# Attention scores split 640 to 640 between the two halves of TensorE's rows, a second use for the value bank, and the even chunks' value products moved behind two later down products

## The chip, the cores and the metric

The kernel runs on one core of a Trainium2 chip. The core has a matrix engine (TensorE, PE in the profile; its weight loads are listed apart as PEld) and three element-wise engines: VectorE (DVE), ScalarE (ACT) and GpSimd (POOL). SyncE (SP) issues all the transfers that matter here. Each engine works through its own list of instructions in order, and engines wait for each other on semaphores. TensorE writes only to PSUM, which has eight banks of 128 partitions by 512 fp32 values. The metric is the device time of one launch in microseconds (us), the median of several runs; lower is better.

## The reference

x is 2048 tokens of 576 features. One half of the model is attention with a compressive memory: 32 heads of 18 features, the sequence cut into four segments of 512 tokens; the other half is a GEGLU feed-forward network with 4608 hidden features. A sigmoid gate per token mixes the two.

```python
for s in range(N):                                   # N = 4 segments of L = 512
    qs, ks, vs = q[:, :, s], k[:, :, s], v[:, :, s]
    logits = jnp.einsum("bhqd,bhkd->bhqk", qs, ks) * scale + mask
    p = _softmax(logits, axis=-1)
    a_dot = jnp.einsum("bhqk,bhkd->bhqd", p, vs)
    ...                                              # memory read: num / den
    o = g * a_mem + (1.0 - g) * a_dot
    outs.append(o)
    ...                                              # memory update
a = concat(outs) @ wo
b = (_gelu(x @ w_gate) * (x @ w_up)) @ w_down
return sigmoid(gate) * a + (1 - sigmoid(gate)) * b
```

The mask is causal inside a segment.

## The kernel before

**Stages.** The first stretch (to about 225 us) projects q, k, v, builds the memories and stores q, k and v in DRAM. The main loop then runs 72 steps (`step(v)`, line 1104), each of some 18.4 us, which carry feed-forward and attention side by side. A tail forms the last down products and the output projection. Every fp32 value is carried as a pair of fp16 words, high and low, so that a product of two values is three matmuls.

**A step's feed-forward part.** Step `v` treats hidden block `f = v // 2` and token pair `p = v % 2`. Gate and up projections of two 512-token chunks are formed with a Strassen-like scheme in three accumulators, each a bank of its own: `V`, `X` (bank `G`) and `Y` (bank `U`). `product` (line 1025) is six matmuls of 512 columns; `rest` (line 1032) and `low_rests` (line 1037) add the last 64 features, the latter with two 64-row products side by side on the two halves of TensorE's rows. Between products, VectorE copies or adds an accumulator (lines 1127, 1130, 1162, 1181, 1189) and ScalarE applies the gelu. `hidden` (line 1007) multiplies gate and up values on VectorE; it is put off to the start of the next step by `end_pair` (line 1096), which goes through the list `ends` (gate accumulator `X` first, then `Y`). A step also makes eight *down products* of the hidden block before (`down`, line 977: six matmuls of 288 columns, line 985, into a `dn` bank, then one VectorE instruction, line 993, that adds the bank to the accumulator `acc`; "eviction" below). Five of them are called `early` (`early[0]` to `early[4]`), three `late`; they stand between the products.

**A step's attention part.** A chunk is one head of one segment: 512 queries by 512 keys. Steps 2 to 65 start two chunks each, the even one `2k` and the odd one `2k + 1`, with `k = v - 2`. `scores` (line 876) forms the causal score rows of a chunk in four blocks of 128 queries: block `qi` sees `(qi + 1) * 128` keys, so its matmul (line 888) has 128, 256, 384 or 512 columns. Queries and keys hold 54 rows (three times 18), and they lie twice in SBUF, at rows 0 and at rows 64, so that one block's product can use the upper half of TensorE's rows while another uses the lower. `put(a, i)` has VectorE add the mask, copy a block out of PSUM and keep the row maximum (line 896). When all blocks are out, ScalarE forms the exponentials (`powers`), ScalarE and GpSimd split them into fp16 pairs (`pair_rows`), and SP turns them by transposing transfers (`turn_rows`, line 926, into `pt`, two buffers). `values(a)` multiplies them with the values, 20 matmuls of 37 columns (line 940) into the bank `pv`; one bank holds the even and the odd chunk of a pair. `normalize` (lines 950 to 957, VectorE) reads it out.

**Order.** The main loop's order on TensorE, VectorE, ScalarE and GpSimd is the order of the calls in `step`; nothing reorders it.

**Banks.** All eight PSUM banks are given out: `G`, `U`, `V` and `pv` once each, `st` and `dn` as pools of two, taken in turn. A tile in a bank waits until the tile before it in the same bank has been read. `spare()` (line 58) gives the down products `dn` in the main loop.

Of the kernel before, what the change touches and what calls it, by code (L numbers as in the profile page):

```python
# [13 lines left out]
OP = mybir.AluOpType  # L14
# [4 lines left out]
P = 128  # L19
# [3 lines left out]
DH = 18  # L23
L = 512
# [18 lines left out]
def kernel(ctx: ExitStack, tc: tile.TileContext, xs, wqk, wv, wo, wgu, wd, beta, out):  # L43
    nc = tc.nc
    pe, act, dve, pool, sp = nc.tensor, nc.scalar, nc.vector, nc.gpsimd, nc.sync
# [6 lines left out]
    def bank(tag, bufs=1, dt=F32):  # L52
        return ps.tile([P, 512 if dt == F32 else 1024], dt, name=tag, tag=tag, bufs=bufs)
# [319 lines left out]
    mask = cst.tile([P, L], BF16, name="mask")  # L373
# [16 lines left out]
    with tc.tile_pool(name="prj", bufs=2, side="right", reuse_waits="tile") as pp:  # L390
# [203 lines left out]
        with tc.manual_schedule(engines=ORDERED):  # L594
# [3 lines left out]
            start = bank("G")  # L598
# [175 lines left out]
            for s in range(4):  # L774
                p = s - 1
                if s:
                    for q in range(4):
                        pv = vrows(s, q, 0)
# [12 lines left out]
                        pv = vrows(s, q, 1)  # L791
# [41 lines left out]
    with tc.tile_pool(name="keep", bufs=2, side="right", reuse_waits="tile") as kp, ExitStack() as tail:  # L833
        home.update(d=kp)
        turns.update(of=2)
        hp, qts, kts, vts, obs, mx, prob = {}, {}, {}, {}, {}, {}, {}
# [34 lines left out]

        COL = [0, P, 3 * P, 6 * P, 10 * P]

        PIECES = (((3,), 0), ((2, 0), 64), ((1,), 0))

        def scores(a):

            k, e = divmod(a, 2)
            q, kt = qts[k], kts[k]
            mx[a] = ap_.tile([P, 4], F32, name="mx", bufs=2)  # L880
            prob[a] = ap_.tile([P, 10 * P], F32, name="pf", bufs=2)
            put = []
            for qis, r in PIECES:
                o = bank("dn", 2) if qis == (1,) else bank("st", 2)
                spots, off, h = [], 0, slice(r, r + 3 * DH)
                for qi in qis:
                    n = (qi + 1) * P
                    pe.matmul(o[:, off : off + n], q[h, e * L + qi * P : e * L + (qi + 1) * P],  # L888
                              kt[h, e * L : e * L + n], start=True, stop=True)
                    spots.append((qi, o[:, off : off + n]))  # L890
                    off += n
                put.append(spots)

            def piece(i):
                for qi, ov in put[i]:
                    dve.tensor_tensor_reduce(prob[a][:, COL[qi] : COL[qi + 1]], ov, mask[:, L - (qi + 1) * P :],  # L896
                                             1.0, -3e38, OP.add, OP.max, mx[a][:, qi : qi + 1])

            return piece

# [27 lines left out]
        def values(a):  # L928
            kk, e = divmod(a, 2)
            if e == 0:  # L930
                pvb[kk] = bank("pv")
            o = pvb[kk]
            pr = turned_p.pop(a)
            v = vts[kk // 4]
            c0 = (kk % 4) * VC
            for qi in range(4):
                ov = o[:, (4 * e + qi) * VC : (4 * e + qi + 1) * VC]
                for kb in range(qi + 1):
                    for i in range(2):
                        pe.matmul(ov, pr[:, 10 * i + COL[qi] // P + kb], v[:, 4 * e + kb, c0 : c0 + VC],  # L940
                                  start=kb == 0 and i == 0, stop=kb == qi and i == 1)
# [62 lines left out]
        def hidden(f, c, o, t):  # L1004

            sc = scl[f // 2][0]
            dve.scalar_tensor_tensor(t, o, sc[:, 6 + c : 7 + c], t, OP.mult, OP.mult)  # L1007
# [86 lines left out]
        ends, puts = [], {}  # L1094

        def end_pair():

            for g in ends:
                hidden(*g)
            for f, c, o, g in ends:  # L1100
                hidden_pair(f, c, g)
            ends.clear()

        def step(v):

            f, p = divmod(v, 2)
            fb, i4 = divmod(v, 4)
            c, e = 2 * p, 2 * p + 1
            k = v - LAG
            on = lambda i: 0 <= i < 2 * H  # L1110
            early = range(8 * i4, 8 * i4 + 5)
            late = range(8 * i4 + 5, 8 * i4 + 8)
            some = lambda b, js: chains(b, js) if b >= 0 else None
            put = lambda a, i: puts[a](i) if a in puts else None
# [11 lines left out]
            g1 = gl_tile()  # L1126
            dve.tensor_copy(g1, V)
            product(X, f, A11, x1, 0, 4, True)
            put(2 * k - 1, 0)
            dve.tensor_copy(Y, X)  # L1130
            if v == 0:
                last_sum(1, 1)
            if v == 1:
                scale_result()
            some(fb - 1, early[:1])
            put(2 * k - 1, 1)
            put(2 * k - 1, 2)
            puts.pop(2 * k - 1, None)
            if on(k - 2):
# [23 lines left out]
            if not fb:  # L1163
                dve.tensor_tensor(g0, V, g0, OP.add)
                gelu(f, c, g0, g0)
            some(fb - 1, early[1:2])
            if v == 0 or fb and i4 == 1:
                scales(fb + 1)
                scales_out(fb + 1)
# [8 lines left out]
                low_rests(f, (V, G4, x1), (Y, G4, x2_))  # L1178
            if on(k):
                puts[2 * k] = scores(2 * k)  # L1180
            dve.tensor_tensor(g1, Y, g1, OP.add)  # L1181
            gelu(f, e, g1, g1)
            if v == 3:
                for n in range(2):
                    high_d(n)
                    low_d(n)
            put(2 * k, 2)
            if fb:
                dve.tensor_tensor(g0, V, g0, OP.add)
                gelu(f, c, g0, g0)  # L1190
            if on(k - 1) and fb:
                values(2 * k - 2)
            some(fb - 1, early[3:4])
            put(2 * k, 0)
            some(fb - 1, early[4:])
            put(2 * k, 1)
            puts.pop(2 * k, None)
            if v < 3:
                ahead[v + 1] = first_product(v + 1)
# [14 lines left out]
            some(fb - 1, late[:1])  # L1214
            if low is not None:
                result_low(low)
            some(fb - 1, late[1:])
            if on(k - 1) and not fb:
                values(2 * k - 2)
            if fb:  # L1220
                low_rests(f, (X, U4, x1), (Y, UG, x2_))
                ends.append((f, c, X, g0))
# [106 lines left out]
```

## Time and profile before

| | |
|---|---|
| device time, median of 3 runs | 1612.17 us (1610.71 to 1613.14) |
| the profiled execution's own time | 1610.65 us |
| its span, first to last instruction | 1608.9 us |
| TensorE busy | 1596.7 us, 99% of the span |
| VectorE / ScalarE / GpSimd busy | 71% / 72% / 70% |
| mean granted TensorE clock | 0.998 |
| score matmuls (line 888) | 512 in 128 chunks |
| value matmuls (line 940) | 2560 in 128 chunks |
| evictions of a `dn` bank (line 993) | 534, mean 516 ns |

Times in the timeline are microseconds from the start of the span. A timeline row gives start, duration, engine, line, operation, the tile written and the tiles read, the shape and the count; where equal instructions follow each other they are merged, and a row's start is that of the first. Brackets at the end give the idle time before the row and what ended it. The end of a matmul is modelled and overlaps the next one's start, so the distance from one matmul's start to the next one's is what TensorE spends on it.

### The profile page before, as it was taken

What the parts mean: (1) busy time and instruction counts of PE and PEld (TensorE: products, weight loads), DVE (VectorE), ACT (ScalarE), POOL (GpSimd) and SP (SyncE); (2) the same over time, 40 slices, a digit from 0 to 9 for tenths busy, and PEclk for the clock granted to TensorE, in tenths of its full rate; (3) what the DMA queues carried; (4) which work ended last, traced back from release to release, by engine and by line L of the source; (5) the groups of instructions that cost most, each with busy time, mean ns of one, the idle gap of its engine ahead of it and who ended that gap; (6) DMA issues with size and microseconds to landing.
All of it is one profiled execution on the core that took longest, in us unless ns stands there. A gap on an engine that the chain in (4) does not pass through costs nothing.

```text
span 1608.9 us, 32610 instructions
## 1 busy us (share of the span) xinstructions
PE 1596.7 (99%) x11924; PEld 933.5 (58%) x11924; DVE 1140.2 (71%) x2940; ACT 1161.9 (72%) x1966; POOL 1133.1 (70%) x1093
## 2 busy tenths in 40 slices
PE   9999999999999999999999999999999999999999
PEld 5656754555555555555555555555555555555577
DVE  6665785677777777777777777777777777765543
ACT  6665445888888888888888888878888888864200
POOL 2233647798987888887979778888879797785200
PEclk9999999999999999999999999999999999999999
DMA  6532443788978797988988887978798887846251
GB/s 240 193 109 77 149 142 82 124 133 131 138 120 141 122 144 120 143 126 140 134 135 133 131 139 123 148 128 141 129 140 137 133 133 129 127 74 155 59 133 60
DMA packets 471872, 209.00 MB, mean 130 GB/s; under 512 B 427552, under 2 KB 436768, under 8 KB 471200
## 3 DMA queue, kind: packets, MB, share of 16 engines
q1 hardware_dynamic: 471712, 206.92, 71.6%
q8 instruction: 94, 1.54, 0.4%
q14 instruction: 66, 0.54, 0.1%
HBM read 90.99 MB, written 27.26 MB: 73 GB/s over the span
## 4 chain that ended last, share of the span: by engine, by line
PE 96%; DVE 1%; DMA 1%; POOL 1%; ACT 1%; issue 0%; SPq 0%; DVEq 0%; POOLq 0%
PE dn L985 26%; PE U L1025 17%; PE V L1025 12%; PE G L1025 11%; PE pv L940 4%; PE st L322 3%; PE st L312 3%; PE dn L322 2%; PE G L312 2%; PE U L1032 2%; PE st L888 2%; PE V L1037 1%; PE G L1037 1%; PE U L312 1%; PE G L1032 1%; PE V L1032 1%
## 5 line engine op out<-in xcount | busy, mean ns | idle before, releaser
L920 POOL TENSOR_TENSOR ph<-pf,ph 128x512 f16<-128x512 f32 (+1 forms) x256 | 354.2, 1405 | 176.9 <-ACT ph L919 175.0
L985 PE MATMUL dn<-paird,hh 128*128 128x288 f16 x3396 | 476.7, 286 | 0.9 <-POOL paird L305 0.9
L1025 PEld LDWEIGHTS <-pairg 128*128 128x128 f16 x3024 | 285.3, 98 | 309.9 <-issue 16.0
L985 PEld LDWEIGHTS <-hh 128*128 128x128 f16 x3456 | 332.3, 98 | 138.1 <-issue 2.6
L993 DVE SCALAR_TENSOR_TENSOR acc<-dn,ev,acc 128x288 f32<-128x288 f32 x534 | 274.0, 516 | 95.7 <-PE dn L985 86.9
L909 ACT ACTIVATE pf<-pf,mb,esc 128x512 f32<-128x512 f32 (+3 forms) x512 | 292.9, 642 | 6.7
L1025 PE MATMUL G<-x,pairg 128*128 128x512 f16 x864 | 209.9, 379 | 0.5 <-DVE gl L1007 0.5
L1025 PE MATMUL U<-xt,pairg 128*128 128x512 f16 x864 | 210.1, 379 | 0.0
L1012 POOL TENSOR_TENSOR hh<-gl,hh 128x512 f16<-128x512 f32 x144 | 164.0, 1160 | 56.0 <-ACT hh L1011 56.0
L896 DVE CUSTOM_DVE_ANT_0 pf<-st,mask 128x512 f32<-128x512 f32 (+2 forms) x384 | 184.0, 504 | 0.0
L293 POOL TENSOR_TENSOR pairg<-raw,pairg 128x640 f16<-128x640 f32 (+2 forms) x144 | 173.9, 1229 | 10.6 <-ACT pairg L289 10.6
L919 ACT ACTIVATE ph<-pf 128x512 f16<-128x512 f32 (+1 forms) x256 | 172.4, 720 | 0.0
L1162 DVE COPY gl<-U 128x512 f32<-128x512 f32 x72 | 49.8, 691 | 137.2 <-PE U L1025 137.2
L289 ACT ACTIVATE pairg<-raw 128x640 f16<-128x640 f32 (+2 forms) x144 | 89.5, 648 | 70.7 <-POOL raw L283 41.2
L258 POOL TENSOR_SCALAR raw<-raw,sc 128x640 f32<-128x640 f32 x72 | 135.0, 1889 | 0.0
L1015 ACT ACTIVATE gl<-gl,sc 128x512 f32<-128x512 f32 x144 | 98.3, 717 | 45.4 <-DVE gl L1181 25.2
L1025 PE MATMUL V<-x,pairg 128*128 128x512 f16 x432 | 106.0, 381 | 0.4 <-ACT hh L1011 0.2
L1181 DVE TENSOR_TENSOR gl<-U,gl 128x512 f32<-128x512 f32 x72 | 49.7, 691 | 79.8 <-PE U L1037 72.5
L1025 PE MATMUL V<-xt,pairg 128*128 128x512 f16 x432 | 105.7, 381 | 0.0
L1025 PE MATMUL U<-x,pairg 128*128 128x512 f16 x432 | 105.0, 379 | 0.4 <-DVE gl L1181 0.4
L1011 ACT ACTIVATE hh<-gl 128x512 f16<-128x512 f32 x144 | 82.9, 616 | 25.2 <-DVE gl L1007 25.1
L906 ACT ACTIVATE mb<-mx,esc 128x4 f32<-128x4 f32 x128 | 37.8, 295 | 85.8 <-DVE mx L896 83.1
(271 smaller groups left out, 2565.1 us busy)
## 6 DMA issues: line engine op xcount, KB each, us to landing
raw<-in_wgu_dram SPq DMA_DIRECT2D x36, 640.0 KB
rawd<-in_wd_dram SPq DMA_DIRECT2D x36, 288.0 KB
qk<-stage SPq DMA_DIRECT2D x36, 256.0 KB
qt<-qk SPq DMA_DIRECT2D x128, 72.0 KB
kt<-qk SPq DMA_DIRECT2D x128, 72.0 KB
vp<-vstage SPq DMA_DIRECT2D x16, 296.0 KB
vt<-vp SPq DMA_DIRECT2D x16, 296.0 KB
qt<-qk SPq DMA_DIRECT2D x128, 36.0 KB
```

The source lines that it names most:

```text
L258: pool.tensor_scalar(r, r, scl[f // 2][0][:, 0:1], None, OP.mult)
L293: pool.tensor_tensor(spot(f, *p, 1), raw_g[f][:, p[0] : p[1]], spot(f, *p, 0), OP.subtract)
L312: pe.matmul(o, w(k, a), x[:, 4 * b + k], start=n == 0, stop=False)
L896: dve.tensor_tensor_reduce(prob[a][:, COL[qi] : COL[qi + 1]], ov, mask[:, L - (qi + 1) * P :], 1.0, -3e38, OP.add, OP.max, mx[a][:, qi : q ...
L909: act.activation(r, r, AF.Exp, bias=b[:, qi : qi + 1], scale=esc[:, 0, c : c + 1])
L919: act.activation(h[:, 0, cols], p[:, cols], AF.Copy)
L920: pool.tensor_tensor(h[:, 1, cols], p[:, cols], h[:, 0, cols], OP.subtract)
L985: pe.matmul(o[:, :NH], hh[:, a, q * P : (q + 1) * P], w[:, b, n * NH : (n + 1) * NH], start=i == 0, stop=i == 5)
L993: dve.scalar_tensor_tensor(av, o[:, :NH], ev, av, OP.mult, OP.add)
L1012: pool.tensor_tensor(hh[:, 1], t, hh[:, 0], OP.subtract)
L1015: act.activation(t, o, AF.Gelu_apprx_tanh, scale=scl[f // 2][0][:, 2 + c : 3 + c])
L1025: pe.matmul(o, w[:, i, (a + k) * P : (a + k + 1) * P], x[:, b + k], start=start and k == 0 and i == 0 and b == h, stop=k == 1 and i == 1, ...
```

## The change

`PIECES` becomes a list of the four blocks with the row half and the bank of each for an even and an odd chunk. The 512-column block stays at rows 0 and the 384-column block at rows 64, each in an `st` bank. The 256-column block goes from rows 0 to rows 64 (bank `dn`, as before). The 128-column block goes from rows 64, where it shared an `st` bank with the 384-column block, to rows 0 and a bank of its own: `pv` in even chunks, `dn` in odd ones. `put` now takes a block's number instead of a piece's.

On VectorE, an odd chunk's 256- and 128-column blocks are read out in `end_pair`, between the two `hidden` instructions that the step before left over; an even chunk's 256-column block is read out ahead of the addition to `g1` (line 1181 before) instead of behind it, its 128-column block behind the addition to `g0`, and its 512- and 384-column blocks where pieces 0 and 1 stood.

On TensorE, `values(2k - 2)` moves from between the score products of chunk `2k` and `early[3]` to between `late[1]` and `late[2]`, from step 4 on. In step 4 alone (the fifth), `early[0]` moves back to stand directly ahead of `early[1]`.

```diff
--- before.py
+++ after.py
@@ -871,7 +871,7 @@
 
         COL = [0, P, 3 * P, 6 * P, 10 * P]
 
-        PIECES = (((3,), 0), ((2, 0), 64), ((1,), 0))
+        PIECES = ((3, 0, "st", "st"), (2, 64, "st", "st"), (1, 64, "dn", "dn"), (0, 0, "pv", "dn"))
 
         def scores(a):
 
@@ -879,22 +879,15 @@
             q, kt = qts[k], kts[k]
             mx[a] = ap_.tile([P, 4], F32, name="mx", bufs=2)
             prob[a] = ap_.tile([P, 10 * P], F32, name="pf", bufs=2)
-            put = []
-            for qis, r in PIECES:
-                o = bank("dn", 2) if qis == (1,) else bank("st", 2)
-                spots, off, h = [], 0, slice(r, r + 3 * DH)
-                for qi in qis:
-                    n = (qi + 1) * P
-                    pe.matmul(o[:, off : off + n], q[h, e * L + qi * P : e * L + (qi + 1) * P],
-                              kt[h, e * L : e * L + n], start=True, stop=True)
-                    spots.append((qi, o[:, off : off + n]))
-                    off += n
-                put.append(spots)
-
-            def piece(i):
-                for qi, ov in put[i]:
-                    dve.tensor_tensor_reduce(prob[a][:, COL[qi] : COL[qi + 1]], ov, mask[:, L - (qi + 1) * P :],
-                                             1.0, -3e38, OP.add, OP.max, mx[a][:, qi : qi + 1])
+            out = {}
+            for qi, r, *tags in PIECES:
+                n, h = (qi + 1) * P, slice(r, r + 3 * DH)
+                out[qi] = bank(tags[e], 1 if tags[e] == "pv" else 2)[:, :n]
+                pe.matmul(out[qi], q[h, e * L + qi * P : e * L + n], kt[h, e * L : e * L + n], start=True, stop=True)
+
+            def piece(qi):
+                dve.tensor_tensor_reduce(prob[a][:, COL[qi] : COL[qi + 1]], out[qi], mask[:, L - (qi + 1) * P :],
+                                         1.0, -3e38, OP.add, OP.max, mx[a][:, qi : qi + 1])
 
             return piece
 
@@ -1097,6 +1090,10 @@
 
             for g in ends:
                 hidden(*g)
+                if g is ends[0]:
+                    for qi in (1, 0):
+                        if puts:
+                            puts[max(puts)](qi)
             for f, c, o, g in ends:
                 hidden_pair(f, c, g)
             ends.clear()
@@ -1126,14 +1123,14 @@
             g1 = gl_tile()
             dve.tensor_copy(g1, V)
             product(X, f, A11, x1, 0, 4, True)
-            put(2 * k - 1, 0)
+            put(2 * k - 1, 3)
             dve.tensor_copy(Y, X)
             if v == 0:
                 last_sum(1, 1)
             if v == 1:
                 scale_result()
-            some(fb - 1, early[:1])
-            put(2 * k - 1, 1)
+            if v != 4:
+                some(fb - 1, early[:1])
             put(2 * k - 1, 2)
             puts.pop(2 * k - 1, None)
             if on(k - 2):
@@ -1163,7 +1160,7 @@
             if not fb:
                 dve.tensor_tensor(g0, V, g0, OP.add)
                 gelu(f, c, g0, g0)
-            some(fb - 1, early[1:2])
+            some(fb - 1, early[0 if v == 4 else 1 : 2])
             if v == 0 or fb and i4 == 1:
                 scales(fb + 1)
                 scales_out(fb + 1)
@@ -1178,22 +1175,21 @@
                 low_rests(f, (V, G4, x1), (Y, G4, x2_))
             if on(k):
                 puts[2 * k] = scores(2 * k)
+            put(2 * k, 1)
             dve.tensor_tensor(g1, Y, g1, OP.add)
             gelu(f, e, g1, g1)
             if v == 3:
                 for n in range(2):
                     high_d(n)
                     low_d(n)
-            put(2 * k, 2)
             if fb:
                 dve.tensor_tensor(g0, V, g0, OP.add)
                 gelu(f, c, g0, g0)
-            if on(k - 1) and fb:
-                values(2 * k - 2)
+            put(2 * k, 0)
             some(fb - 1, early[3:4])
-            put(2 * k, 0)
+            put(2 * k, 3)
             some(fb - 1, early[4:])
-            put(2 * k, 1)
+            put(2 * k, 2)
             puts.pop(2 * k, None)
             if v < 3:
                 ahead[v + 1] = first_product(v + 1)
@@ -1214,9 +1210,10 @@
             some(fb - 1, late[:1])
             if low is not None:
                 result_low(low)
-            some(fb - 1, late[1:])
-            if on(k - 1) and not fb:
+            some(fb - 1, late[1:2])
+            if on(k - 1):
                 values(2 * k - 2)
+            some(fb - 1, late[2:])
             if fb:
                 low_rests(f, (X, U4, x1), (Y, UG, x2_))
                 ends.append((f, c, X, g0))
```

## The prediction

> **What bounds the kernel now.** First the page: how busy each engine is, then the chain of work that ended last, then the busy time by stretches and the list of who waited for whom.
>
> ```profile
> span 1608.9 us, 32610 instructions
> PE 1596.7 (99%) x11924; PEld 933.5 (58%) x11924; DVE 1140.2 (71%) x2940; ACT 1161.9 (72%) x1966; POOL 1133.1 (70%) x1093
> ...
> PE 96%; DVE 1%; DMA 1%; POOL 1%; ACT 1%; issue 0%; SPq 0%; DVEq 0%; POOLq 0%
> ```
>
> ```profile
> 260.00:300.00 40.00, 36.78 (x243) 17.86 (x243) 23.15 (x67) 33.89 (x57) 28.27 (x23) 0.96 0.63 120
> 300.00:600.00 300.00, 300.00 (x2395) 170.99 (x2394) 226.69 (x618) 253.13 (x425) 251.15 (x232) 1.00 0.84 131
> ```
>
> ```profile
> PE pv L940 <- DMA pt<-ph: 1.7, 2, 0.9
> PE dn L985 <- POOL paird L305: 0.9, 2, 0.7
> PE U L1025 <- DVE gl L1181: 0.4, 1, 0.4
> ```
>
> TensorE is the bound: 96% of the chain that ended last, and from 300 us on it is busy for all of 300 us out of 300. Its waits in the loop are a few, all before 300 us (the second fence has 36.78 of 40 there). So a nanosecond taken from TensorE's list is a nanosecond of the kernel, and so is one that it is made to wait. What counts is the distance between starts of its matmuls. The timeline of one even chunk, in a step of the settled loop:
>
> ```profile
> 845.50 0.38 PE L888 MATMUL st<-kt,qt 54*128 54x512 f16 x3
> 845.71 0.69 DVE L1181 TENSOR_TENSOR gl<-U,gl 128x512 f32<-128x512 f32 x1 [1.32 <-PE U L1037]
> 845.72 0.27 PE L888 MATMUL dn<-kt,qt 54*128 54x256 f16 x1
> 845.92 0.68 PE L940 MATMUL pv<-vt,pt 128*128 128x37 f16 x20
> 846.32 0.41 DVE L896 CUSTOM_DVE_ANT_0 pf<-dn,mask 128x256 f32<-128x256 f32 x1
> 846.45 1.63 PE L985 MATMUL dn<-paird,hh 128*128 128x288 f16 x12
> 846.66 0.69 DVE L1189 TENSOR_TENSOR gl<-V,gl 128x512 f32<-128x512 f32 x1
> 847.92 1.46 PE L1025 MATMUL U<-x,pairg 128*128 128x512 f16 x6
> 849.21 0.38 PE L1032 MATMUL U<-x,pairg 128*128 128x512 f16 x1
> ```
>
> The scores take 845.92 - 845.50 = 0.42 us of TensorE. Six products of 512 columns take 849.21 - 847.92 = 1.29 us, 0.215 each, or 0.42 ns a column. So the halves do run side by side: the `dn` block (256 columns, rows 0) starts 0.22 after the first, which is the 512 columns of rows 0 alone, while the 384 and the 128 columns of rows 64 fit beside them. The last 0.20 is 256 columns (0.107) and 0.093 for going back to products over all rows.
>
> The same chunk pair's odd half, with VectorE beside it:
>
> ```profile
> 851.10 0.52 DVE L993 SCALAR_TENSOR_TENSOR acc<-dn,ev,acc 128x288 f32<-128x288 f32 x1 [0.22 <-PE dn L985]
> 851.87 0.52 DVE L993 SCALAR_TENSOR_TENSOR acc<-dn,ev,acc 128x288 f32<-128x288 f32 x1 [0.25 <-PE dn L985]
> 851.99 0.38 PE L888 MATMUL st<-kt,qt 54*128 54x512 f16 x3
> 852.21 0.27 PE L888 MATMUL dn<-kt,qt 54*128 54x256 f16 x1
> 852.30 0.74 DVE L1007 SCALAR_TENSOR_TENSOR gl<-G,sc,gl 128x512 f32<-128x512 f32 x1
> 852.41 1.47 PE L1025 MATMUL V<-xt,pairg 128*128 128x512 f16 x6
> 852.96 0.74 DVE L1007 SCALAR_TENSOR_TENSOR gl<-U,sc,gl 128x512 f32<-128x512 f32 x1
> 853.71 1.46 PE L1025 MATMUL G<-x,pairg 128*128 128x512 f16 x6
> 853.98 0.69 DVE L1127 COPY gl<-V 128x512 f32<-128x512 f32 x1 [0.28 <-PE V L1025]
> ```
>
> Here the reader is to see the eviction of the third late product: it waits for TensorE (0.25 idle), starts 0.12 before the scores and ends at 852.39, that is 0.40 after their start. Today nobody needs that bank so soon: the one `dn` block takes the other bank, whose eviction ended at 851.62.
>
> **The even chunk.** New loads of the halves: 512 + 128 = 640 columns on rows 0, 384 + 256 = 640 on rows 64. The last block starts at 0.22 and lasts 128 x 0.42 ns = 0.054; the 256 columns start at 384 x 0.42 = 0.16 and end at 0.27 too. With 0.093 for the way back: 0.37 in place of 0.42, a gain of **0.05 us**. It needs its bank `pv`: the one before in it is read by `normalize`, and VectorE has nothing to do for 1.32 us ahead of 845.71, so that is over; bounds of this wait 0 and 0.
>
> On VectorE the 256-column copy now stands ahead of the Y addition. It can start when its block is out (start 0.16 + 0.27 in the record = 0.43 after the scores began) and holds VectorE 846.66 - 846.32 = 0.34, the addition its 0.69: done at 1.46. Behind the addition waits the product into `U`, at 847.92 now. With `values(2k - 2)` gone from here it comes at 0.37 + two down products (847.92 - 846.45 = 1.47) = 1.84. So 0.38 is left, less a hand-over; cost nothing. If that cover were gone, every 0.1 us missing would cost 6 us over the loop. The second of these down products takes the bank of the 256 columns: free at 0.85, needed at 1.10. ScalarE's gelu comes 0.6 us later and the row maxima end about when they did.
>
> `values` itself costs 846.45 - 845.92 = 0.53 wherever full-row products surround it, so its move is free; its transfers get some 5 us more, and its `pt` buffer is needed again only by the next even chunk's transposes, behind that chunk's exponentials.
>
> **The odd chunk.** Both small blocks are now in `dn`, which has two banks. The block of 256 takes the one of `late[1]`, evicted long since, with `values` in between. The block of 128 takes the one of `late[2]`, the product that ends right ahead of `low_rests` and the scores. The instruction order of the changed program, as built, says the same: in 62 of the 64 odd chunks this matmul waits for the eviction of the down product whose last matmul is six matmuls before it. `values` stands ahead of `late[2]`, not behind it, so it gives this eviction no time. The eviction's length hardly varies:
>
> ```profile
> L993 DVE SCALAR_TENSOR_TENSOR acc<-dn,ev,acc x534: 505/517/520, 359.3 to 1601.9; 128x288 f32<-128x288 f32 x178
> ```
>
> In one pair out of four, where `result_low` (line 969) stands between the late evictions, it ends a little later, 815.61 against scores that begin at 815.14:
>
> ```profile
> 814.67 0.94 DVE L993 SCALAR_TENSOR_TENSOR acc<-dn,ev,acc 128x288 f32<-128x288 f32 x2
> ...
> 815.14 0.38 PE L888 MATMUL st<-kt,qt 54*128 54x512 f16 x3
> ```
>
> There `values` ahead of `late[2]` gives VectorE the time to catch up, so I take 0.40 for all; the matmul could start at 0.22. The hand-over from VectorE to a waiting TensorE is in the two rows where that happens today:
>
> ```profile
> 273.33 0.69 DVE L1181 TENSOR_TENSOR gl<-U,gl 128x512 f32<-128x512 f32 x1 [1.97 <-PE U L1032]
> ...
> 274.08 1.46 PE L1025 MATMUL U<-x,pairg 128*128 128x512 f16 x6 [0.36 <-DVE gl L1181]
> ...
> 277.67 0.75 DVE L1007 SCALAR_TENSOR_TENSOR gl<-G,sc,gl 128x512 f32<-128x512 f32 x1 [2.01 <-ACT gl L1015]
> ...
> 278.47 1.46 PE L1025 MATMUL G<-x,pairg 128*128 128x512 f16 x6 [0.19 <-DVE gl L1007]
> ...
> 281.46 0.41 PE L985 MATMUL dn<-paird,hh 128*128 128x288 f16 x2 [0.71 <-POOL paird L305]
> ...
> 282.73 0.69 PE L940 MATMUL pv<-vt,pt 128*128 128x37 f16 x19 [0.84 <-DMA pt<-ph]
> 283.25 2.72 PE L1025 MATMUL V<-x,pairg 128*128 128x512 f16 x6
> 285.77 0.63 PE L1032 MATMUL V<-x,pairg 128*128 128x512 f16 x1
> ...
> 294.10 0.64 PE L940 MATMUL pv<-vt,pt 128*128 128x37 f16 x19 [0.89 <-DMA pt<-ph]
> ```
>
> 274.08 - 274.02 and 278.47 - 278.42: 0.05 to 0.06. So the block starts at 0.455, and the product `V` behind it, which TensorE takes in order though its bank and operands are ready, at 0.455 + 0.054 + 0.093 = 0.60 instead of 0.42: **0.18 us lost** in place of 0.05 gained. Bounds: at best the bank is handed over when VectorE takes its next instruction (852.30, 0.31): lost 0.04 to 0.09. At worst the eviction ends at 0.47 and more in every pair: 0.28.
>
> [...] No run here shows a matmul passing another, and the starts above are in order.
>
> Behind it on VectorE: the first `hidden` starts with the eviction's end, as now (852.30), then come the two copies (0.34 and about 0.2), so the second `hidden`, the copy of `V` (853.98) and of `U` come up to 0.55 later. The next to need them is the product that adds to `V`, two products, a down product and `values` later (2.59 + 0.73 + 0.53 after 852.41: 856.3, against 855.3 for the copy's end). Free.
>
> **The fifth pair (step 4).** Today TensorE waits for `early[0]`'s weights (0.71), then for the odd chunk's transposed scores, which land at 282.73 whatever TensorE does, and it then runs at half clock (six products in 283.25 to 285.77, 2.52 instead of 1.29). In the change `early[0]` no longer fills that wait: it costs its 0.73 later. Against that `values(2k - 2)` stands later and its 0.89 wait goes. Step 3's addition, with no down products as cover, stalls longer, but ends in the same wait for the transfer. I take 0; bounds -1 and +2 (another stretch at half clock).
>
> **Sum.** 62 x 0.18 = 11.2; 66 x -0.05 = -3.3 (64 even, 2 odd chunks before any down product); start 0. Together **+7.9 us**. The profiled execution took 1610.65 (span 1608.9), so 1618.6; the median of the runs is 1.5 above that execution, hence 1620.
>
> **Rivals.**
>
> 1. *The bank is free in time (faster).* If the eviction's release reached TensorE by 852.21, all 128 chunks would gain 0.05: -6.4, **1605.8**. For it: VectorE starts its next instruction at 852.30 already. Against: even that is 0.09 late, and in both hand-overs above TensorE went on after the full record. Deciding point: 0.18 us. Chance 0.10.
> 2. *The halves don't share.* If the 128 columns of rows 0 wait until the 256 of rows 64 are through, an even chunk takes 0.27 + 0.054 + 0.093 = 0.42 as before: only 11.2 is left, **1623**. Against: the 256 columns at 845.72 start when their own rows are free. Chance 0.08.
> 3. *VectorE becomes late in the even half.* If the cover of 0.38 fails by 0.2 in each step, 64 x 0.2 = 12.8 more: **1633**. For it: the addition stalled TensorE 0.36 where no down product stood between. Chance 0.06.
> 4. *The clock.* If each stall cost one stretch like that at 283.25 (about 1.2 us lost in its six products), 62 x 1.2 = 74: **1694**. Against: the clock stood at 1.00 from 300 to 600, and the drop followed waits of 0.71 and 0.84 close together, not one of 0.2 in 18 us. Chance 0.01. [...]
>
> **How the numbers follow.** The forecast has 0.75. Its own range: 62 x 0.065 (the middle of 0.04 to 0.09, the earliest release) - 3.3 = +0.7, up to 62 x 0.28 + 2 - 3.3 = +16: 1613 to 1628. Rival 2 lies inside; 1, 3 and 4 stay out with 0.17. About 0.2%, 3 us, is what a measurement can tell from no change. Slower by more: 0.75 + 0.08 + 0.06 + 0.01, less 0.06 for the early release: 0.84. Within: 0.06. Faster: 0.10.
>
> **What would show it.** In the list of waits a new row, TensorE's `dn` at the score line waiting for VectorE's eviction, some 62 times, 0.2 us each, 14 us in all. The distance from an odd chunk's first score to `V` 0.60, from an even chunk's to the down product 0.37. The values' 0.89 wait gone. Wrong I would be if odd chunks took 0.37 (rival 1), even ones 0.42 (2), the products into `U` waited for the addition (3), or the clock fell below 0.99 (4).

## The result, and the profile after

| | before | after |
|---|---|---|
| device time, median of 13 runs each | 1612.07 us (1610.71 to 1613.47) | 1614.80 us (1614.19 to 1616.45) |
| ratio of the times | 1 | 1.0019, interval 1.0011 to 1.0026 |
| the profiled execution's own time / span | 1610.65 / 1608.9 us | 1614.53 / 1612.8 us |
| mean granted TensorE clock of that execution | 0.998 | 1.000 |

The change makes the kernel slower by 2.7 us. The forecast was +7.9: right in sign, and the time lies in the range, but the size is about a third of what was said.

The page of the changed kernel: its span, and its engines' busy time, share and instructions.

```profile
span 1612.8 us, 32563 instructions
...
PE 1598.9 (99%) x11924; PEld 932.8 (58%) x11924; DVE 1127.9 (70%) x2940; ACT 1158.3 (72%) x1966; POOL 1131.8 (70%) x1093
```

The same two stretches as before, busy time by engine:

```profile
260.00:300.00 40.00, 36.26 (x252) 18.00 (x251) 24.77 (x74) 35.31 (x60) 28.23 (x23) 1.00 0.62 120
300.00:600.00 300.00, 299.79 (x2385) 170.50 (x2384) 222.43 (x612) 250.88 (x422) 251.00 (x232) 1.00 0.82 131
```

TensorE remains the bound and looks as full as before, yet it now starts 2385 matmuls in the second stretch and not 2395. The busy share does not see what happened. The starts do. One pair of chunks of the changed kernel in the settled loop, TensorE and VectorE:

```profile
846.49 0.38 PE L886 MATMUL st<-kt,qt 54*128 54x512 f16 x2
846.66 0.27 PE L886 MATMUL dn<-kt,qt 54*128 54x256 f16 x1
846.71 0.21 PE L886 MATMUL pv<-kt,qt 54*128 54x128 f16 x1
846.86 1.65 PE L978 MATMUL dn<-paird,hh 128*128 128x288 f16 x12
848.34 1.46 PE L1018 MATMUL U<-x,pairg 128*128 128x512 f16 x6
...
849.86 1.63 PE L978 MATMUL dn<-paird,hh 128*128 128x288 f16 x12
851.33 0.67 PE L933 MATMUL pv<-vt,pt 128*128 128x37 f16 x20
851.84 0.90 PE L978 MATMUL dn<-paird,hh 128*128 128x288 f16 x6
...
852.77 0.52 DVE L986 SCALAR_TENSOR_TENSOR acc<-dn,ev,acc 128x288 f32<-128x288 f32 x1 [0.73 <-PE dn L978]
852.89 0.38 PE L886 MATMUL st<-kt,qt 54*128 54x512 f16 x2
853.06 0.49 PE L886 MATMUL dn<-kt,qt 54*128 54x256 f16 x2
853.21 0.74 DVE L1000 SCALAR_TENSOR_TENSOR gl<-G,sc,gl 128x512 f32<-128x512 f32 x1
853.49 1.47 PE L1018 MATMUL V<-xt,pairg 128*128 128x512 f16 x6
```

The even chunk's scores take 846.86 - 846.49 = 0.37 us (0.42 before). The odd chunk's take 853.49 - 852.89 = 0.60 (0.42 before): the eviction of `late[2]` ends at 852.77 + 0.52 = 853.29, and only then can the odd chunk's second `dn` block start, the row at 853.06 holding both. The distances between starts, averaged over the 59 pairs from chunk 8 to chunk 126:

| piece of a pair (start to start, us) | before | after |
|---|---|---|
| scores of the even chunk | 0.419 | 0.369 |
| the two down products `early[3]` and `early[4]` | 1.467 | 1.481 |
| `values(2k - 2)` | 0.520 | 0.508 |
| three late down products and the way to half rows | 2.335 | 2.298 |
| scores of the odd chunk | 0.419 | 0.596 |
| sum of these | 5.160 | 5.252 |

That is +0.092 a pair, 59 x 0.092 = 5.4; the distance from chunk 8's first score product to chunk 126's went from 1085.19 to 1090.53, +5.34. From chunk 126 to the end both kernels take 193.2 to 193.3. So what makes the rest must lie before chunk 8, as both reach chunk 0 at 261.36 and 261.35 us: from chunk 0's first score product to chunk 8's, 69.13 us before and 67.61 after, -1.5. Rows of that start, changed kernel:

```profile
275.24 1.46 PE L1018 MATMUL U<-x,pairg 128*128 128x512 f16 x6 [1.24 <-DVE gl L1179]
...
281.97 0.19 PE L933 MATMUL pv<-vt,pt 128*128 128x37 f16 x1 [1.28 <-DMA pt<-ph]
283.10 0.64 PE L933 MATMUL pv<-vt,pt 128*128 128x37 f16 x19 [0.93 <-DMA pt<-ph]
283.59 1.46 PE L1018 MATMUL V<-x,pairg 128*128 128x512 f16 x6
284.88 0.38 PE L1025 MATMUL V<-x,pairg 128*128 128x512 f16 x1
...
296.77 0.66 PE L933 MATMUL pv<-vt,pt 128*128 128x37 f16 x20
```

Step 3's addition stalls TensorE 1.24 (0.36 before), the odd chunk's values wait 1.28 and 0.93; but the six products behind them run at full speed, 284.88 - 283.59 = 1.29, where they took 2.52 before, and the values of chunk 2, which waited 0.89 before, do not wait at all at 296.77.

The changed kernel's list of waits, in us, times and the longest:

```profile
PE pv L933 <- DMA pt<-ph: 2.2, 2, 1.3
...
PE U L1018 <- DVE gl L1179: 1.2, 1, 1.2
```

All of TensorE's waits above are there; the 62 waits of the odd chunks are in no row, although each is 0.2 us long. The reason is in the timeline: a matmul's modelled end (852.89 + 0.38 = 853.27 for the blocks ahead) runs on over the wait. Waits of TensorE as short as these 0.2 us are seen here in the distances between starts alone.

### The profile page after: what moved, and what is told of

Read it like the earlier page. It is cut to its first block, busy times and chain, and to the rows that moved or that the text cites. A ratio compares the mean times of both kernels' runs of the same rounds, so it can differ in the third digit from the quotient of the medians.

```text
span 1612.8 us, 32563 instructions
## 1 busy us (share of the span) xinstructions
PE 1598.9 (99%) x11924; PEld 932.8 (58%) x11924; DVE 1127.9 (70%) x2940; ACT 1158.3 (72%) x1966; POOL 1131.8 (70%) x1093
## 4 chain that ended last, share of the span: by engine, by line
PE 97%; DVE 1%; POOL 1%; DMA 1%; ACT 0%; issue 0%; SPq 0%; DVEq 0%; POOLq 0%
PE dn L978 26%; PE U L1018 17%; PE V L1018 12%; PE G L1018 11%; PE pv L933 4%; PE st L322 3%; PE st L312 3%; PE dn L322 2%; PE U L1025 2%; PE G L312 2%; PE dn L886 2%; PE V L1030 1%; PE G L1030 1%; PE U L312 1%; PE st L886 1%; PE G L1025 1%
## 5 line engine op out<-in xcount | busy, mean ns | idle before, releaser
L978 PE MATMUL dn<-paird,hh 128*128 128x288 f16 x3396 | 485.1, 286 | 0.0
L978 PEld LDWEIGHTS <-hh 128*128 128x128 f16 x3456 | 327.5, 98 | 147.7 <-issue 17.9
L889 DVE CUSTOM_DVE_ANT_0 pf<-st,mask 128x512 f32<-128x512 f32 (+1 forms) x256 | 156.9, 613 | 0.0
L889 DVE CUSTOM_DVE_ANT_0 pf<-dn,mask 128x256 f32<-128x256 f32 (+1 forms) x192 | 67.1, 374 | 88.3 <-PE dn L886 88.3
L933 PEld LDWEIGHTS <-pt 128*128 128x128 f16 x2560 | 83.4, 96 | 9.2 <-DMA pt<-ph 2.8
```

Of the source, the lines that this page charges most:

```text
L978: pe.matmul(o[:, :NH], hh[:, a, q * P : (q + 1) * P], w[:, b, n * NH : (n + 1) * NH], start=i == 0, stop=i == 5)
```

## The experiments

Two theories stood against each other from the start. A: the scores cost what was forecast (+0.18, -0.05), and something else in the pair and in the start gives back; above all `values` now stands where it hides a wait that no list shows. B: the wait in the odd chunk is not the cause, the new layout of the halves costs by itself. Rivals for single edits are named where their runs stand. "Chunk 0 to 8" below is the start, "chunk 8 to 126" the settled loop, both from the first score product of the one to that of the other.

| kernel | median (us) | ratio to before, interval | span | chunk 0 to 8 | chunk 8 to 126 |
|---|---|---|---|---|---|
| before | 1612.07 | 1 | 1608.9 | 69.13 | 1085.19 |
| before, once more | one run, 1613.14 | | 1611.4 | 71.90 | 1085.14 |
| after | 1614.80 | 1.0019 (1.0011 to 1.0026) | 1612.8 | 67.61 | 1090.53 |
| after, once more | one run, 1614.18 | | 1612.5 | 67.55 | 1090.54 |
| e1 | 1602.79 | 0.9944 (0.9931 to 0.9956) | 1600.9 | 67.19 | 1078.82 |
| e2 | 1614.92 | 1.0017 (1.0009 to 1.0026) | 1611.3 | 66.77 | 1090.28 |
| e3 | one run, 1605.80 | | 1604.1 | 68.99 | 1080.18 |
| e4 | 1601.41 | 0.9929 (0.9915 to 0.9942) | 1599.7 | 68.91 | 1076.79 |
| e5 | one run, 1614.07 | | 1612.3 | 66.99 | 1090.54 |
| e6 | one run, 1628.98 | | 1627.3 | 71.61 | 1100.67 |
| e9 | 1611.66 | 0.9992 (0.9983 to 1.0001) | 1609.4 | 69.75 | 1085.15 |
| e10 | one run, 1605.83 | | 1604.1 | 66.69 | 1083.18 |
| e11 | 1599.96 | 0.9922 (0.9909 to 0.9936) | 1597.4 | 66.43 | 1076.83 |

**e1, the values behind the third late product.** The changed kernel with one call moved:

```diff
-            some(fb - 1, late[1:2])
+            some(fb - 1, late[1:])
             if on(k - 1):
                 values(2 * k - 2)
-            some(fb - 1, late[2:])
```

> The changed kernel with one edit: values(2k-2) stands behind the third late down product instead of ahead of it. Theory A (the odd chunk's loss is the wait of the 128-column block for the eviction of the down product right ahead; the values' move also took away a hidden 0.04 us wait of the third late product for the first one's eviction): an odd chunk's scores go from 0.596 to 0.37 us, 62 x 0.227 = -14.1; the three late down products, without values between them, take 0.04 more again, +2.3; span 1612.8 - 11.8 = 1601.0, ratio to the kernel before about 0.995. Rival B (the 0.596 is the price of the new layout itself, of putting the small blocks on two halves and two dn banks): the odd chunk stays at 0.596 and the span at 1612.8 or 2 above.

The timeline of e1:

```profile
295.74 2.40 PE L978 MATMUL dn<-paird,hh 128*128 128x288 f16 x18
...
297.98 0.66 PE L933 MATMUL pv<-vt,pt 128*128 128x37 f16 x20
298.18 0.52 DVE L984 TENSOR_SCALAR acc<-dn,ev 128x288 f32<-128x288 f32 x1 [0.25 <-PE dn L978]
...
298.80 0.38 PE L886 MATMUL st<-kt,qt 54*128 54x512 f16 x2
298.97 0.27 PE L886 MATMUL dn<-kt,qt 54*128 54x256 f16 x2
299.17 1.47 PE L1018 MATMUL V<-xt,pairg 128*128 128x512 f16 x6
```

The eviction of `late[2]` ends at 298.70, before the scores begin, and the odd chunk takes 299.17 - 298.80 = 0.37. The same layout, the same banks, and 0.23 us less: the wait was the whole loss, and B falls. The price is where A put it: the three late products take 297.98 - 295.74 = 2.24, while the three of the changed kernel take 1.47 + 0.735 = 2.205; the wait hidden before is back. The loop loses 11.7 us against the changed kernel, the time 12.0 between the two medians.

**e2, the values' move alone.** The kernel before with only this:

```diff
-            if on(k - 1) and fb:
-                values(2 * k - 2)
             some(fb - 1, early[3:4])
...
-            some(fb - 1, late[1:])
-            if on(k - 1) and not fb:
+            some(fb - 1, late[1:2])
+            if on(k - 1):
                 values(2 * k - 2)
+            some(fb - 1, late[2:])
```

> The kernel before with one part of the change alone: values(2k-2) between the second and third late down product; blocks, banks and VectorE's order as before. Theory A: the three late products lose a wait of 0.037 us a pair, 62 x 0.037 = -2.3; in step 4 the 0.89 us wait of values for its transposes goes, -1.0; span 1608.9 - 3.3 = 1605.6 if the stretch at half clock near 283 us stays, ratio 0.998. Rival B (TensorE waits nowhere for late evictions before, as its list of waits says; the 5.7 us of the settled loop come from somewhere in the scores): the late products keep 2.335 us a pair, and only the 1.0 of step 4 goes, ratio 0.9994.

A miss by 5.7 us of span, although the half-clock stretch near 283 us, with which that span was reckoned, did not come in this profile. The late products did what was expected (2.298, -0.037 a pair), but `early[3]` and `early[4]` went from 1.467 to 1.602. The timeline of e2:

```profile
290.91 0.69 DVE L1181 TENSOR_TENSOR gl<-U,gl 128x512 f32<-128x512 f32 x1 [1.32 <-PE U L1037]
290.92 0.27 PE L888 MATMUL dn<-kt,qt 54*128 54x256 f16 x1
291.12 1.77 PE L985 MATMUL dn<-paird,hh 128*128 128x288 f16 x12
291.52 0.41 DVE L896 CUSTOM_DVE_ANT_0 pf<-dn,mask 128x256 f32<-128x256 f32 x1
...
292.73 1.46 PE L1025 MATMUL U<-x,pairg 128*128 128x512 f16 x6
```

`early[4]` takes the bank of the 256-column block, which is copied out behind the addition: ready at 291.52 + 0.41 = 291.93, wanted at 291.12 + 0.735 = 291.855. With the hand-over that is 0.13 us in each of the 59 pairs, +8.0. Before, `values` stood there and covered it with its 0.52. So the move alone is not free: it needs the earlier copy that comes with the new layout.

**e10, the values' move with the earlier copy, old layout.** e2 with the copy of the 256-column block ahead of the addition:

```diff
+            put(2 * k, 2)
             dve.tensor_tensor(g1, Y, g1, OP.add)
             gelu(f, e, g1, g1)
...
-            put(2 * k, 2)
```

> The kernel before with the values' move and with VectorE's copy of the even 256-column block ahead of the Y addition; score blocks and banks as before. Theory A (this copy is what pays for the values' move): the two down products behind the even scores take 1.47 to 1.48 us in place of 1.60 with the values' move alone, odd scores 0.42, the three late products and values 2.81; loop from chunk 8 to 126 1085.2 - 59 x 0.035 = 1083.1. Rival D (the 1.60 comes from something other than the bank of the 256-column block): 1090.

```profile
291.38 1.64 PE L985 MATMUL dn<-paird,hh 128*128 128x288 f16 x12
291.59 0.42 DVE L896 CUSTOM_DVE_ANT_0 pf<-dn,mask 128x256 f32<-128x256 f32 x1 [1.75 <-PE dn L888]
...
292.86 1.46 PE L1025 MATMUL U<-x,pairg 128*128 128x512 f16 x6
```

In this timeline of e10 the copy ends at 292.01, before `early[4]` needs the bank at 292.115, and the two products take 292.86 - 291.38 = 1.48. The loop is 1083.18 as worked out (1083.1), 2.0 below the kernel before. The one run is 6.7 below the median of before taken beside it, 1612.48; by the profiles, what is more than the loop's 2.0 lies ahead of chunk 8 (66.69, against 69.13 and 71.90), where this one has no half clock (granted clock 1.000). The order alone, without any new sharing of halves, is a gain.

**e3, the odd chunks' blocks as before.** The changed kernel with the old layout in odd chunks: three blocks as before, the 128 columns at rows 64 in the `st` bank of the 384.

```diff
-            for qi, r, *tags in PIECES:
+            pieces = ((3, 0, "st"), (2, 64, "st"), (0, 64, ""), (1, 0, "dn")) if e else [p[:3] for p in PIECES]
+            for qi, r, tag in pieces:
...
```

> The changed kernel with odd chunks' blocks laid out as before (384 and 128 columns on rows 64 in one st bank, 256 on rows 0 in dn); even chunks, VectorE's order and the values' place as changed. Theory A: odd scores 0.42 in place of 0.596, 62 x 0.177 = -11.0, span 1601.8; even scores stay at 0.37. Rival B (the loss comes with VectorE's new order, the small copies between the two hidden instructions): the span stays within 2 us of 1612.8.

Odd scores 0.419, loop 1080.18, that is 10.35 less than the changed kernel, and 59 x (0.596 - 0.419) = 10.4. The span missed its number by 2.3, of which 1.7 is a stretch at half clock that the changed kernel's two profiles do not have: from the first product into `V` behind the waits to the next down product it takes 288.54 - 284.05 = 4.49, in the changed kernel 286.39 - 283.59 = 2.80. The term for the odd chunks stands as forecast.

**e6, the copy behind the addition.** The changed kernel with the 256-column copy of the even chunk moved back:

```diff
-            put(2 * k, 1)
             dve.tensor_tensor(g1, Y, g1, OP.add)
             gelu(f, e, g1, g1)
+            put(2 * k, 1)
```

> The changed kernel with VectorE's copy of the even chunk's 256-column block put back behind the Y addition, where it stood before. Theory A (values, when it stood between the scores and the early down products, covered the wait of early[4] for this dn bank; with values gone only the earlier copy covers it): the two down products behind the even scores take 1.60 us instead of 1.48, as in the run with the values' move alone, 59 x 0.12 = +7 in the loop from chunk 8 to 126, 1097.6. Rival D (the copy's place is free either way, as the prediction costed it): 1090.5.

The two down products take 1.653 in place of 1.481, more than the 1.60 expected, and the loop 10.1 more. It is the wait of e2 again, seen from the other side; the copy's early place is needed. That it is 0.05 longer than in e2 fits the shorter scores: they take 0.369 here and 0.419 in e2, so `early[4]` wants the bank 0.05 sooner, while the copy still comes behind the addition. The start is worse too, 71.61: the odd chunk's values wait 2.99 and 0.96 us there, and the products behind them run at half clock: the six into `V` take 287.36 - 284.84 = 2.52 and the six into `U` 290.21 - 287.79 = 2.42, where either six take 1.29 in the changed kernel.

**e4, one full-row product between the late ones.** e1's order, and the one matmul of `rest` (line 1025) put between `late[1]` and `late[2]`, to cover the wait that came back:

```diff
-            rest(Y, f, UG, x2_, (0,) if fb else (0, 1))
+            if not fb:
+                rest(Y, f, UG, x2_)
             some(fb - 1, late[:1])
...
             some(fb - 1, late[1:2])
+            if fb:
+                rest(Y, f, UG, x2_, (0,))
+            some(fb - 1, late[2:])
             if on(k - 1):
                 values(2 * k - 2)
-            some(fb - 1, late[2:])
```

> The changed kernel with values(2k-2) behind the third late down product, and the 512-column rest into U (0.216 us) moved from ahead of the first late product to between the second and the third. Theory A: both waits are gone, the odd chunk's block (0.37) and the hidden one of the third late product, which now gets 0.2 us more than it needs: span 1612.8 - 14.1 = 1598.7, ratio about 0.9935, faster than both kernels. Rival B (the first late product, 0.2 us earlier, then waits for its own bank, or VectorE is late with the first eviction): 0.05 to 0.2 a pair is lost again, 1602 to 1611.

The timeline of e4:

```profile
298.10 0.38 PE L1025 MATMUL U<-x,pairg 128*128 128x512 f16 x1
298.32 0.90 PE L978 MATMUL dn<-paird,hh 128*128 128x288 f16 x6
299.05 0.66 PE L933 MATMUL pv<-vt,pt 128*128 128x37 f16 x20
```

`late[2]` comes 0.22 later than right behind `late[1]`, at no cost, since that matmul had to be made anyway, and takes its plain 0.73. The loop is 1076.79, 2.0 under e1's: 0.034 a pair, the whole hidden wait. The median is 1.4 under e1's, with overlapping intervals; the loop's distance is the sharper measure.

**e5, without the fifth pair's reordering.** The changed kernel with `early[0]` in its old place in step 4:

```diff
-            if v != 4:
-                some(fb - 1, early[:1])
+            some(fb - 1, early[:1])
...
-            some(fb - 1, early[0 if v == 4 else 1 : 2])
+            some(fb - 1, early[1:2])
```

> The changed kernel without the swap in step 4: early[0] stands ahead of the odd values again, as in every other step. Theory A (the odd chunk's transposed scores land near 283 us whatever TensorE does, so a down product ahead of them is free): the first score product of chunk 8 starts 0.7 us earlier after the landing than with the swap, span -0.7; the settled loop from chunk 8 to 126 stays at 1090.5. Rival C (the swap is what kept the clock up, 1.000 against 0.998 before): the profile has a stretch of 3.4 us at half clock again near 283 us, and the span grows by 1.7 - 0.7 = 1.0.

The start takes 66.99, 0.6 less than in the changed kernel, and no stretch ran at half clock in this one profile (granted clock 1.000). So the move of `early[0]` costs about 0.6 us, if one profile of a start can be trusted so far. Rival C, by which it keeps the clock up, finds no support here, nor in the last table of this document: 4 of 13 runs of the changed kernel, which has that move, show a clock below 1.000, and none of the 5 of e11, which has not.

**e7 and e8, both kernels once more.** No edit.

> The kernel before, once more, for the spread between executions. [...] Rival C (the half clock belongs to the kernel before): it is there again, at 283.1.

> The changed kernel, once more, for the spread between executions. Theory A: the loop from chunk 8 to 126 is 1090.5 again within 0.1; a stretch at half clock near 283 us may appear, with 1.7 us more ahead of chunk 8. Rival C (the swap in step 4 keeps the clock up): no half clock ahead of the tail.

The loops repeat to 0.05 us (table). The starts do not: the kernel before took 71.90 where its first profile had 69.13. In e7 the values of chunk 2 wait longer, and the half clock comes behind them, at 295.98 and not at 283.10. So it does not belong to one place of the kernel before:

```profile
293.83 0.19 PE L940 MATMUL pv<-vt,pt 128*128 128x37 f16 x1 [1.49 <-DMA pt<-ph]
294.93 0.64 PE L940 MATMUL pv<-vt,pt 128*128 128x37 f16 x19 [0.90 <-DMA pt<-ph]
```

So the start of the changed kernel is 1.5 to 4.3 us shorter, by which profile of before it is held against, and the difference of the two spans is no better than that.

**e9, the values' move in step 4 alone.** The kernel before with `values(2)` late in step 4 and all else as it was:

```diff
-            if on(k - 1) and fb:
+            if on(k - 1) and fb and v != 4:
                 values(2 * k - 2)
...
-            some(fb - 1, late[1:])
-            if on(k - 1) and not fb:
+            some(fb - 1, late[1:2])
+            if on(k - 1) and (not fb or v == 4):
                 values(2 * k - 2)
+            some(fb - 1, late[2:])
```

> The kernel before with the values' later place in step 4 alone; all other steps, the score blocks, the copies and early[0] as before. Theory A (the change's gain at the start is this one move: the even values no longer wait for their transposes near 294 us, 1.0 us in one profile and 2.4 in the other, and a window at half clock, 1.7, comes less often): the time from chunk 0 to chunk 8 falls from 69.1 and 71.9 to some 67.3, the loop from chunk 8 to 126 stays at 1085.2, ratio to the kernel before 0.9975 to 0.999. Rival C (the start's difference was chance or the swap of early[0]): 69 or more from chunk 0 to chunk 8, ratio 1.000.

The median is 0.8 below before, and the interval just reaches 1, nearer to what rival C said. The start took 69.75 and not 67.3: this profile too has a half-clock stretch (the six products into `U` take 289.28 - 286.88 = 2.40), behind waits of 0.71, 1.39 and 0.94 us up to the values of chunk 1. The wait of `values(2)` is gone, but something as large waits earlier. What this one move is worth stays open.

**e11, the best order found.** e4 without the fifth pair's reordering (the diffs of e4 and e5 together).

> The version with both waits gone (values behind the third late product, the rest into U between the second and the third), without the swap in step 4: early[0] fills TensorE's wait for the odd chunk's transposes again. Theory A: chunk 0 to chunk 8 0.6 us shorter than with the swap, loop 1076.8 as in that version, span 1597.5 to 1599.2 by the clock near 283 us; ratio to the kernel before about 0.9925. Rival C (early[0] ahead of that wait costs what it saves): ratio 0.993 and no shorter start.

1599.96 us, faster than both kernels: 12.5 below the 1612.48 of before taken beside it. Its loop equals e4's to 0.04, and its start, 66.43, is the shortest of all: 2.5 less than in e4, of which 1.7 is the half clock at 283.9 in e4's profile.

## Why the prediction was right, and where it was wrong

The forecast of +7.9 was 5.2 us too high. Two terms that the prediction put at nothing make the difference: the move of `values`, with which the loop gave back some 2.2 us, and the start, which gave back some 3.0 us. The first is shown by the runs; of the second a part stays open.

**The scores: right, term for term.** The even chunk gained 0.050 (forecast 0.05), the odd chunk lost 0.177 (forecast 0.18). The mechanism was the one described: e1 takes the wait away with the layout kept, and the odd chunk falls to 0.369, as the even one; e3 takes the layout away with the order kept, and the odd chunk goes back to 0.419. Rivals 1 and 2, a bank free in time and halves that do not share, are both refuted by the table of a pair. TensorE did not let `V` pass the waiting block: the eviction that the block waits for ends at 853.29, and `V` starts at 853.49, behind the block.

**`values`: wrong.** The step that failed is "so its move is free". It looked at the 0.53 that `values` takes and asked whether its inputs and buffers were ready; it did not ask what the place between `late[1]` and `late[2]` was doing. It had read from the busy share and the list of waits that TensorE's waits in the loop are "a few, all before 300 us", and that is not so. The rows of the kernel before that were passed over:

```profile
849.43 2.40 PE L985 MATMUL dn<-paird,hh 128*128 128x288 f16 x18
...
850.37 0.52 DVE L993 SCALAR_TENSOR_TENSOR acc<-dn,ev,acc 128x288 f32<-128x288 f32 x1 [0.75 <-PE dn L985]
```

With two `dn` banks, `late[2]` uses the bank of `late[0]`. Its eviction ends at 850.37 + 0.52 = 850.89, and with the 0.05 of a hand-over `late[2]` can start at 850.94. By the products' own length it would start at 849.43 + 2 x 0.735 = 850.90. So it waited 0.04 us, and the pairs' mean says that this was so throughout the loop; it is in no list. Three late products and the switch should take 3 x 0.735 + 0.093 = 2.298; before they took 2.335, after they took 2.298. With `values` in between the wait is gone, in the changed kernel and, with the old layout, in e2: 62 x -0.037 = -2.3. The other side of the same step, what `values` covered at its old place, cost nothing only because the copy had been moved too; e2 shows 0.135 a pair without that, and the prediction's reason for the copy (the bank free at 0.85, needed at 1.10) held.

**VectorE late in the even half (rival 3): did not happen.** The two down products took 1.481, 0.014 more than before, not 0.2.

**The start: taken as 0 with bounds of -1 and +2, measured -1.5 to -4.3.** The waits went as described: the addition of step 3 stalls longer (1.24), the transposes of the odd chunk are waited for longer (2.2 for 0.84, which `early[0]` no longer fills), and the 0.89 of `values(2)` is gone. What was mis-sized is the half clock: the prediction quoted the six products that take 2.52 in place of 1.29, but counted another such stretch as a risk and not the loss of this one as a gain. One stretch is worth 1.7 us in the changed kernel's runs. By the last table below, how often it comes makes some 1.1 to 1.6 of the 3.0 us that the start gave back; what makes the rest stays open, since two profiles of the same kernel differ by 2.8 us here.

**The sum.** Forecast 11.2 - 3.3 + 0 = 7.9. By the table of a pair: 62 x (0.177 - 0.050) = 7.9 for the scores, 62 x (-0.037 - 0.012 + 0.014) = -2.2 for the late products, the values and the early products, together 5.7. The medians differ by 2.7, so the start is left with about -3.0, inside its two readings of -1.5 and -4.3.

**What would show it: one item wrong.** The prediction said that the waits of the odd chunks would make a row of the list. They do not; the distances 0.60 and 0.37, which it also named, were the right place to look.

## What to carry to other kernels

When work is moved on the bounding engine, ask of both places what it was covering there: an eviction that ended just as its bank was wanted made a wait of 0.04 us here, which the list of waits did not show and which cost 2.3 us over 62 pairs. Find such waits by adding up what the products should take and holding it against the distance of their starts. With two banks in turn, put other work between the last product and the next user of its bank (one matmul put there in e4 took 2.0 us off the loop of e1), and let the copy that frees a bank go ahead of work that nobody waits for (behind it, in e6, the loop took 10.1 us more).

## What the runs showed of the hardware

**The half clock.** In three profiles the stretch with the lower clock was looked at by itself: 283.10 to 286.51 us in the first profile of before, 283.90 to 287.31 in e4, 295.98 to 299.40 in e7. Each time TensorE's granted clock was 0.50 for 3.41 to 3.42 us. The kernel before, then the changed kernel, in the same two stretches; the column behind the busy times is the granted clock:

```profile
279.60:283.10 3.50, 1.77 (x24) 1.00 (x23) 2.48 (x10) 3.41 (x6) 2.92 (x3) 1.00 0.97 192
283.10:286.51 3.41, 3.41 (x19) 1.28 (x16) 0.35 (x3) 2.74 (x6) 2.10 (x2) 0.50 0.70 216
```

```profile
279.60:283.10 3.50, 1.29 (x8) 0.39 (x5) 2.67 (x10) 3.41 (x7) 3.29 (x3) 1.00 1.05 218
283.10:286.51 3.41, 3.41 (x33) 1.85 (x34) 0.00 (x0) 2.96 (x6) 1.74 (x2) 1.00 0.69 216
```

Before, TensorE stood still for 1.73 of 3.50 us and the next 3.41 ran at 0.50. After, it stood still for more, 2.21 us, and the clock stayed at 1.00. So the sum of the waits does not tell the two apart. The table has TensorE's waits of 0.5 us or more between 279 and 285 us, and what the first six products of 512 columns into `V` and into `U` behind them took from start to start. In the changed kernel, where the clock stood at 1.00, six take 1.29 us:

| profile | waits (us) | six products into `V` (us) | six products into `U` (us) |
|---|---|---|---|
| before | 0.71, 0.84 | 285.77 - 283.25 = 2.52 | 287.65 - 286.19 = 1.46 |
| e9 | 0.71, 1.39, 0.94 | 286.45 - 284.79 = 1.66 | 289.28 - 286.88 = 2.40 |
| e3 | 1.27, 0.93 | 285.96 - 284.05 = 1.91 | 288.54 - 286.39 = 2.15 |
| e4 | 1.29, 0.93 | 285.38 - 283.38 = 2.00 | 287.87 - 285.81 = 2.06 |
| e6 | 2.99, 0.96 | 287.36 - 284.84 = 2.52 | 290.21 - 287.79 = 2.42 |
| after | 1.28, 0.93 | 284.88 - 283.59 = 1.29 | 286.39 - 285.10 = 1.29 |
| e1 | 1.26, 0.93 | 285.32 - 284.03 = 1.29 | 286.83 - 285.54 = 1.29 |
| e2 | 0.71, 0.96 | 284.38 - 283.09 = 1.29 | 285.89 - 284.59 = 1.30 |
| e7 | 0.70, 0.99, 0.96 | 285.53 - 284.24 = 1.29 | 287.04 - 285.75 = 1.29 |

In e7 the lower clock came behind two later waits, of 1.49 and 0.90 us: the two down products there took 297.74 - 295.42 = 2.32 (1.47 in the loop), the six products into `U` 299.86 - 297.74 = 2.12.

In the changed kernel and in e1 the products kept their 1.29 us, in e3 and e4 they did not, behind waits that differ by 0.03 us at most. The first profile of before lost the full clock behind 0.71 and 0.84 us, and e7, the same kernel, kept it behind 0.70, 0.99 and 0.96. So the lengths of these waits alone do not tell the two cases apart either; what does is not shown by these runs.

**How often it comes.** Each profile with such a stretch shows a mean granted clock of 0.998 or 0.999, each without shows 1.000. By this mark, over the timed runs whose clock is on record (e7, e8 and the first profile of before, single runs, are left out):

| kernel | runs | below 1.000 | median of these (us) | median of those at 1.000 (us) |
|---|---|---|---|---|
| before | 31 | 29 | 1612.4 | 1610.2 |
| after | 13 | 4 | 1616.24 | 1614.53 |
| e2 | 11 | 5 | 1616.7 | 1613.08 |
| e9 | 11 | 10 | 1611.7 | 1608.88 |
| e11 | 5 | 0 | | 1599.96 |

In the changed kernel the two kinds of run lie 1616.24 - 1614.53 = 1.7 us apart, the price of one stretch (half of 3.41). In e2 they lie 3.7 apart, more than the 1.7 of one stretch; what the rest is stays open, since no profile of such a run of e2 was taken. Held against before at the same mark, the changed kernel is 1614.53 - 1610.2 = 4.3 us slower (only two runs of before) or 1616.24 - 1612.4 = 3.8. The medians differ by 2.7, because the median run of before has a stretch and the median run of after has none. So 1.1 to 1.6 of the 3.0 us that the start gave back comes from how often such a stretch comes. Which of the edits to the start makes the stretch rarer is not settled: the values' late place in step 4 alone left it in 10 of 11 runs, and the kernel without the fifth pair's reordering was run five times only as e11, where the order of the late products differs too.
